# A fused attention and feed-forward kernel: its first batch gets a schedule of its own

## Chip, cores and metric

One core of a Trainium2 chip runs the kernel. The metric is the device time of one execution in microseconds, the median of repeated runs. Engines are called by the profile's names: PE is TensorE, DVE is VectorE, ACT is ScalarE, POOL is GpSimd, SP is SyncE, which here only issues DMAs.

## What is computed

Four batches (B = 4) of 448 positions (S), 12 heads (H) of 64 (D), in float32. Cut to what matters:

```python
scores = scale * np.matmul(q, k.transpose(0, 1, 3, 2))
scores = np.where(mask, -1000000000.0, scores)
scores = scores - np.max(scores, axis=-1, keepdims=True)
attn = np.exp(scores)
attn = attn / (np.sum(attn, axis=-1, keepdims=True) + 1e-09)
x = concat_heads(np.matmul(attn, v))
mu, var = mean(x), mean((x - mu) ** 2)
xn = (x - mu) / np.sqrt(var + 1e-06) * g_ln
out = x + np.maximum(xn @ w_ch1, 0.0) @ w_ch2
```

The mask is causal; the widths are 768 (x), 3072 (hidden) and 768.

## The kernel before

**The feed-forward part** (`ffn`) multiplies in three products of a rounded format: each weight tile is split into a high part `wh` and a rest `wl`, each input into `xh` and `xl` (later `hh` and `hl`), and `wh*xh`, `wh*xl` and `wl*xh` are summed in PSUM (L421, L440). It runs over 48 weight tiles a batch, in an order of slots: one slot is half of a pair of matmul groups. Weight tiles arrive packed; in the first batch ACT unpacks each with two instructions (L99, L103), DVE joins them (L110), ACT makes `wh` (L122) and DVE `wl` (L126), and the joined tile is kept in DRAM for the later batches (L117). All of these are the *conversions* of a tile.

**The attention part** works on pairs of heads (p = 0 to 5). Per pair: scores of row blocks of 112 (L227 for the first batch in plain float32, L234 for the others in rounded parts), a DVE instruction that adds the mask, scales and finds the row minimum of the negated scores (L242), ACT's exponential with row sums (L256), the normalization (r on DVE, L267 and L268, then four multiplications a head, L272), transposes of the probability blocks on PE into PSUM tile `pt` (L288), their copies to `PT` by ACT (L291) or DVE (L293), and the product with the values, `px` (L303), copied to `xT` (L307). When all six pairs are done, means and variances are taken (`stats`, L316 and L319; `aggr`), spread over the partitions by matmuls into `mb` and `rb` (`spread`, L336 and L341), and `xg`, `xh` and `xl` are made (L351 to L361).

**What sets the order.** Each engine runs its instructions in the order of the program, which is written out by slot numbers: `steps` puts each step of pair p at slot 6p plus a table value (SAT0 for scores, one slot later the exponentials, NAT0 for the normalization, TAT0 for transposes, END0 for the value product, TH0 for statistics). Attention of batch 1 to 3 runs in the slots of the feed-forward part of the batch before it; attention of batch 0 runs ahead of everything, in negative slots (the *head* below). EARLY, GAP and ELAG place the conversions of the first four weight tiles in the head. For batch 1, HOLE and FIRST pull the first steps into the head: the loads, splits and scores of its first pair.

In the head the queries and keys of a pair lie as three planes: head 0 in rows 0 to 63 with zeros below, head 1 in rows 64 to 127 with zeros above, and the keys of both; POOL writes the zeros (L171, L172). A scores matmul so runs over 128 rows, half of them zero. PSUM has eight banks, three named sc, two mm, two pt, one pv; scores of the head take turns over sc and mm. DMAs are all issued from SP's queue.

Of the kernel before, what the change touches and what calls it, by code (L numbers as in the profile page):

```python
# [40 lines left out]
NDVE = 7  # L41
# [6 lines left out]
def kernel(ctx, tc, qk, v, w1, w2, g, out):  # L48
# [108 lines left out]
    class Att:  # L157
# [47 lines left out]
        def scores(self, p, grp):  # L205
            if self.b == 0:
                tag, bufs = (("sc", 3), ("sc", 3), ("sc", 3), ("mm", 2), ("mm", 2))[self.turn % 5]
                self.turn += 1
            else:
                tag, bufs = "sc", 3  # L210
# [3 lines left out]
            for h, i in grp:  # L214
                n = C * (i + 1)
                if ("P", p, h) not in self.t:
                    x = 2 * p + h
                    if self.b == 0 and x % 5 >= 3:
                        a = 2 * NC * D * NP + (x % 5 - 3) * OFF[NC]
                        old = (x - 5) // 2, (x - 5) % 2  # L220
                        assert x < 5 or all(("T", *old, j) in self.done for j in range(NC))
                        self.t["P", p, h] = rest[:C, a:a + OFF[NC]]
                    else:
                        self.t["P", p, h] = sb.tile([C, OFF[NC]], F32, tag="P", name="P", bufs=3)
                if self.b == 0:
                    r = self.t["raw", p]
                    nc.tensor.matmul(  # L227
                        pt[:, o:o + n], lhsT=r[:, h, C * i:C * i + C], rhs=r[:, 2, :n],
                        start=True, stop=True,
                    )  # L230
                else:
                    qs, kh, kl = self.t["qk", p]
                    for kk, part in ((kh, 0), (kl, 1)):
                        nc.tensor.matmul(  # L234
                            pt[:, o:o + n], lhsT=qs[:, h, C * i:C * i + C], rhs=kk[:, h, :n],
                            start=(part == 0), stop=(part == 1),
                        )
# [12 lines left out]
        def exps(self, p, grp):  # L250
            nm = self.t.pop(("nm", p, tuple(grp)))
            for x, (h, i) in enumerate(grp):
                if ("sm", p, h) not in self.t:
                    self.t["sm", p, h] = sb.tile([C, NC], F32, tag="sm", name="sm", bufs=6)
# [7 lines left out]
        def norm(self, p, h):  # L262
# [6 lines left out]
            eng = nc.vector if self.b or p >= NDVE else nc.gpsimd  # L269
            for i in (0, 1, 3, 2):  # L270
                pp = self.t["P", p, h][:, OFF[i]:OFF[i + 1]]
                eng.tensor_scalar(  # L272
# [75 lines left out]
        def apply1(self, c):  # L348
# [4 lines left out]
            )  # L353
            nc.vector.scalar_tensor_tensor(
# [11 lines left out]
        def steps(self):  # L366
# [6 lines left out]

            if self.b == 0:
                sat, tat, nat, end, ev = SAT0, TAT0, NAT0, END0, EV0
            else:
                sat, tat, nat, end, ev = SAT, TAT, NAT, END, EV1 if self.b == 1 else EV
            period = 6
            for p in range(NP):
                t0 = period * p  # L380
                if self.b:
# [3 lines left out]
                for h in range(2):  # L385
                    put(pre, t0 + nat[h], self.norm, p, h)
                put(post, t0 + end, self.pv, p)
                for x, grp in enumerate(TGROUPS):
                    put(post, t0 + tat[x], self.transposes, p, grp, "act" if ev[x] else "dve")
                for x, grp in enumerate(SGROUPS):  # L390
                    put(post, t0 + sat[x], self.scores, p, grp)
                    put(pre, t0 + sat[x] + 1, self.exps, p, grp)
# [9 lines left out]
            for c in range(KC):  # L402
                x = c if self.b else c // 2
                put(pre, ta + 1 + x, self.apply1, c)
# [4 lines left out]
    def ffn(a, s, hh, hl):  # L409
        for f0, f1 in ((0, HF), (HF, NF)):  # L410
            for x in range(0, HF, 2):
# [4 lines left out]
                for k, (y, c) in enumerate(seq):  # L416
# [3 lines left out]
                    for i, (w, z) in enumerate(((wh[ws], a.xh), (wh[ws], a.xl), (wl[ws], a.xh))):  # L420
# [29 lines left out]
    with tc.manual_schedule():  # L450
        more_qk = sb.tile([P, KC, S], F32, tag="xh", name="more_qk", bufs=1)
        first_qk = sb.tile([P, HF, S], F32, tag="hh", name="first_qk")
        rest = sb.tile([P, HF * S], F32, tag="hl", name="rest")
        pre, post, att = {}, {}, {}

        def add_batch(b):
# [32 lines left out]
        for s in range(start, B * ns):  # L489
            for b in range(1, B):  # L490
                if b not in att and s >= (b - 1) * ns - (-start if b == 1 else 8):
# [49 lines left out]
```

## Time and profile before

| | before |
|---|---|
| median of 3 runs | 918.5 us (918.12 to 918.62) |
| the profiled execution, its own time | 920.24 us |
| span in its profile | 918.4 us |
| busy share of the span | PE 98%, DVE 60%, ACT 49%, POOL 13% |
| chain that ended last, by engine | PE 87%, ACT 6%, DVE 5% |
| first feed-forward matmul | starts at 79.18 us |

The profile is of one execution; times in it count from the start of its span. Busy time of PE is the modelled length of matmuls that overlap each other, so a PE row that is long may follow the last one sooner than its length says: the distance between starts is what counts. The granted clock is that of PE, 1.00 for 2.4 GHz and 0.50 for 1.2 GHz.

### The profile page before, as it was taken

Reading aid. Unit: us, or ns where it says so; the run is one execution under the profiler, and the core shown is the slowest. Engines: PE = TensorE matmul, PEld = TensorE weight load, DVE = VectorE, ACT = ScalarE, POOL = GpSimd, SP = SyncE. Lnnn points to the kernel's source line nnn. Section 1 sums busy time; section 2 is a strip of 40 time slices with the busy share of each in tenths; the row PEclk is TensorE's granted clock in tenths of the full one; section 3 lists DMA queues with packets and bytes.
Section 4 is the critical chain, followed back from the end, with each engine's and each line's share of the span. In section 5 each row is a group of like instructions: output and inputs, shape, how many; then the busy total and the mean of one; then the engine's idle time right before and its main releaser. Section 6 shows DMA issues by size and latency. Waiting matters only on the chain.

```text
span 918.4 us, 12826 instructions
## 1 busy us (share of the span) xinstructions
PE 897.3 (98%) x4864; PEld 790.0 (86%) x4864; DVE 554.0 (60%) x1208; ACT 452.8 (49%) x907; POOL 121.6 (13%) x115
## 2 busy tenths in 40 slices
PE   6988999999999999999999999999999999999998
PEld 4656889888899988988889998888988999999997
DVE  4877678777778566655664676556664634333431
ACT  5955788778865444444432355433542333222320
POOL 5543111001022111100102210011100200000000
PEclk9999999999999999999999999999999999999999
DMA  9921778887778643333213634343222343323210
GB/s 236 345 78 34 274 253 285 285 304 244 257 253 273 238 153 110 105 128 119 98 50 125 215 126 150 120 151 112 84 95 77 121 146 117 121 103 103 103 65 31
DMA packets 35247, 144.36 MB, mean 157 GB/s; under 512 B 4081, under 2 KB 8689, under 8 KB 35185
## 3 DMA queue, kind: packets, MB, share of 16 engines
q1 hardware_dynamic: 35184, 143.54, 45.3%
q8 instruction: 38, 0.62, 0.3%
q14 instruction: 25, 0.20, 0.1%
HBM read 119.15 MB, written 24.38 MB: 156 GB/s over the span
## 4 chain that ended last, share of the span: by engine, by line
PE 87%; ACT 6%; DVE 5%; DMA 1%; issue 1%; SPq 1%; POOL 0%; ACTq 0%
PE po L440 38%; PE ph L421 33%; PE px L303 5%; PE sc L234 4%; PE pt L288 4%; ACT P L256 2%; PE pln L316 1%; DMA raw<-w_dram 1%; ACT w L99 1%; ACT bits L103 1%; PE sc L227 1%; DVE hl L427 1%; ACT wh L122 1%; DVE P L272 1%; DVE wl L126 1%
## 5 line engine op out<-in xcount | busy, mean ns | idle before, releaser
L421 PE MATMUL ph<-xh,wh 128*128 128x448 f32 x576 | 214.5, 372 | 2.2 <-ACT xh L358 1.4
L440 PE MATMUL po<-hh,wh 128*128 128x448 f32 x576 | 214.1, 372 | 0.0
L421 PE MATMUL ph<-xl,wh 128*128 128x448 f32 x576 | 211.7, 367 | 0.8 <-POOL xl L361 0.8
L421 PE MATMUL ph<-xh,wl 128*128 128x448 f32 x576 | 211.5, 367 | 0.2
L440 PE MATMUL po<-hh,wl 128*128 128x448 f32 x576 | 210.7, 366 | 0.0
L440 PE MATMUL po<-hl,wh 128*128 128x448 f32 x576 | 210.6, 366 | 0.0
L427 DVE SCALAR_TENSOR_TENSOR hl<-ph,hh 128x448 fp32r<-128x448 f32 x96 | 59.9, 624 | 147.1 <-ACT hh L426 147.1
L122 ACT ACTIVATE wh<-full 128x768 fp32r<-128x768 f32 x144 | 119.3, 838 | 53.7 <-PE po L440 50.8
L126 DVE TENSOR_TENSOR wl<-full,wh 128x768 fp32r<-128x768 f32 x144 | 136.4, 954 | 0.8 <-ACT wh L122 0.5
L426 ACT ACTIVATE hh<-ph 128x448 fp32r<-128x448 f32 x96 | 52.0, 543 | 154.2 <-PE ph L421 154.1
L256 ACT ACTIVATE P<-P,nm 112x448 f32<-112x448 f32 (+3 forms) x176 | 91.8, 524 | 68.0 <-DVE nm L242 68.0
L421 PEld LDWEIGHTS ph<-xh,wh 128*128 128x128 f32 x576 | 108.7, 189 | 11.2 <-ACT xh L358 1.6
L421 PEld LDWEIGHTS ph<-xh,wl 128*128 128x128 f32 x576 | 108.6, 189 | 10.6 <-DVE wl L126 2.1
L421 PEld LDWEIGHTS ph<-xl,wh 128*128 128x128 f32 x576 | 108.7, 189 | 9.0 <-POOL xl L361 1.1
L440 PEld LDWEIGHTS po<-hh,wl 128*128 128x128 f32 x576 | 108.2, 188 | 9.3 <-DVE wl L126 0.4
L440 PEld LDWEIGHTS po<-hh,wh 128*128 128x128 f32 x576 | 108.2, 188 | 8.5
L440 PEld LDWEIGHTS po<-hl,wh 128*128 128x128 f32 x576 | 108.3, 188 | 8.1
L203 POOL TENSOR_TENSOR kl<-qkraw,kh 128x896 fp32r<-128x896 f32 x18 | 51.8, 2877 | 378.5 <-DVE kh L193 378.5
L242 DVE CUSTOM_DVE_ANT_0 P<-sc,mask 112x448 f32<-112x448 f32 (+3 forms) x176 | 70.6, 445 | 51.9 <-PE sc L234 39.7
L444 DVE TENSOR_TENSOR xT<-po,xT 128x448 f32<-128x448 f32 x48 | 29.9, 624 | 112.2 <-PE po L440 112.2
L288 PE MATMUL pt<-ident,P 112*112 112x112 f32 x440 | 55.3, 262 | 4.1 <-ACT PT L291 3.0
L288 PEld LDWEIGHTS pt<-ident,P 112*112 112x112 f32 x440 | 47.1, 134 | 13.9 <-ACT PT L291 4.6
(63 smaller groups left out, 940.6 us busy)
## 6 DMA issues: line engine op xcount, KB each, us to landing
full<-scratch SPq DMA_DIRECT2D x72, 768.0 KB, 4.3
raw<-w_dram SPq DMA_DIRECT2D x48, 768.0 KB, 5.6
scratch<-w SPq DMA_DIRECT2D x48, 384.0 KB, 2.9
qkraw<-qk_dram SPq DMA_DIRECT2D x18, 896.0 KB, 7.4
out_dram<-xT SPq DMA_DIRECT2D x24, 224.0 KB, 2.0
vt<-v_dram SPq DMA_DIRECT2D x18, 224.0 KB, 5.2
first_qk<-qk_dram SPq DMA_DIRECT2D x8, 224.0 KB, 5.9
rest<-v_dram SPq DMA_DIRECT2D x6, 224.0 KB, 8.2
```

Of the source, the lines that this page charges most:

```text
L122: nc.scalar.activation(out=wh[s], in_=w32[s], func=ACTF.Copy)
L126: nc.vector.tensor_tensor(out=wl[s], in0=w32[s], in1=wh[s].bitcast(F32), op=ALU.subtract)
L203: nc.gpsimd.tensor_tensor(out=kl, in0=rk, in1=kh.bitcast(F32), op=ALU.subtract)
L234: nc.tensor.matmul(pt[:, o:o + n], lhsT=qs[:, h, C * i:C * i + C], rhs=kk[:, h, :n], start=(part == 0), stop=(part == 1),)
L242: nc.vector.tensor_tensor_reduce(out=self.t["P", p, h][:, OFF[i]:OFF[i + 1]], in0=pt[:, o:o + n], in1=mask[:, S - n:], op0=ALU.add, op1=AL ...
L256: nc.scalar.activation(out=pp, in_=pp, func=ACTF.Exp, scale=-1.0, bias=nm[:, x:x + 1], accum_out=self.t["sm", p, h][:, i:i + 1],)
L288: nc.tensor.transpose(pt[:, o:o + C], pp[:, a:a + C], ident[:C, :C])
L303: nc.tensor.matmul(px[D * h:D * h + D, C * j:], lhsT=vt[:, h, j, :], rhs=self.t.pop(("PT", p, h, j)), start=(j == 0), stop=(j == NC - 1),)
L421: nc.tensor.matmul(pm[y], lhsT=w[:, c * P:c * P + P], rhs=z[:, c, :], start=(c == 0 and i == 0), stop=(c == KC - 1 and i == 2),)
L426: nc.scalar.activation(out=hh[:, x + y, :], in_=pm[y], func=ACTF.Relu)
L427: nc.vector.scalar_tensor_tensor(out=hl[:, x + y, :], in0=pm[y], scalar=0.0, in1=hh[:, x + y, :].bitcast(F32), op0=ALU.max, op1=ALU.subtract,)
L440: nc.tensor.matmul(pm, lhsT=w[:, o:o + P], rhs=z[:, x, :], start=(x == 0 and i == 0), stop=(x == HF - 1 and i == 2),)
```

## The change

1. First batch, scores: the zero planes and POOL's 12 memsets go. Head 0 lies in rows 0 to 63 and head 1 in rows 64 to 127 (queries and keys, two planes), and each scores matmul (L222 of the changed kernel) runs over its 64 rows; the two heads alternate and write two different PSUM tiles. The groups are block 3, blocks 0 and 2, block 1, of both heads.
2. First batch, order: new tables. One normalization for both heads (`norm0`) at slot 7 instead of two at slots 4 and 6, with r of 112x8; transposes from slot 9, value product at 14. A sixth buffer for probabilities (`more_p`). The second head of the last pair is normalized on DVE.
3. Conversions of the first four weight tiles: from slots -45, -39, -33, -27 to -15, -12, -9, -6, and closer to each other (ELAG).
4. Batch 1 loses HOLE and FIRST: all its steps stand where those of batches 2 and 3 stand, so its first pair's loads, splits and scores come after the start of the feed-forward part, and its other steps three slots later.
5. `apply1` is cut into `center` and `apply`; in batch 0 two centerings come ahead of two scalings. The second and third product of L421 change places.

```diff
-HOLE = [-7, 1]
-EARLY = 45
-GAP = 6
-FIRST = -20
-SAT0, TAT0, NAT0, END0, EV0 = [-1, 0, 2, 2, 4], [7, 8, 9, 10, 11], [4, 6], 13, [1, 1, 0, 1, 0]
+EARLY = 15
+GAP = 3
+GROUPS0 = [[3], [0, 2], [1]]
+SAT0, TAT0, NAT0, END0, EV0 = [0, 2, 4], [9, 9, 11, 11, 12], 7, 14, [0, 1, 0, 1, 0]
-TH0, TH = [38, 40], [18, 30]
-ELAG = [2, 5, 7]
+TH0, TH = [27, 39], [18, 30]
+ELAG = [1, 2, 3]
...
-                r = (first_qk if p < 4 else more_qk)[:, p % 4 * 3:p % 4 * 3 + 3, :]
-                nc.gpsimd.memset(r[D:, 0, :], 0.0)
-                nc.gpsimd.memset(r[:D, 1, :], 0.0)
-                nc.sync.dma_start(out=r[:D, 0:3:2, :], in_=qk[0, p][:D, 0:3:2, :])
-                nc.sync.dma_start(out=r[D:, 1:3, :], in_=qk[0, p][D:, 1:4:2, :])
+                r = first_qk[:, 2 * p:2 * p + 2, :]
+                nc.sync.dma_start(out=r[:D], in_=qk[0, p][:D, 0:3:2, :])
+                nc.sync.dma_start(out=r[D:], in_=qk[0, p][D:, 1:4:2, :])
...
+                for h in range(2):
+                    nc.tensor.matmul(
+                        tiles[h][:, o:o + n], lhsT=r[D * h:D * h + D, 0, C * i:C * i + C],
+                        rhs=r[D * h:D * h + D, 1, :n], start=True, stop=True,
+                    )
...
+        def norm0(self, p):
+            sm = self.t.pop(("sm", p))
+            r = sb.tile([C, 2, NC], F32, tag="r0", name="r0", bufs=2)
+            nc.vector.tensor_scalar_add(r, sm, 1e-9)
+            nc.vector.reciprocal(r, r)
+            for h in range(2):
+                eng = nc.vector if p == NP - 1 and h == 1 else nc.gpsimd
+                for i in (0, 1, 3, 2):
+                    eng.tensor_scalar(
...
-                    for i, (w, z) in enumerate(((wh[ws], a.xh), (wh[ws], a.xl), (wl[ws], a.xh))):
+                    for i, (w, z) in enumerate(((wh[ws], a.xh), (wl[ws], a.xh), (wh[ws], a.xl))):
...
-                if b != 1:
-                    return t + shift
-                if t < 0:
-                    return t + FIRST
-                return t - 2 + HOLE[0] if t <= 2 else t - 3 + HOLE[1]
+                return t + shift
```

**Place 1: DVE, from the transposes of one pair to the normalization of the next.** In the changed kernel, with `pt_237` and `pt_251` the last transposes of pair 0, `sc_258` and `sc_259` the first scores of pair 2, and `r0_266` the normalization of pair 1:

```order
L338 COPY PT_214<-pt_213 112x448
L232 ISA P_175,nm_231<-sc_227,mask_67 112x224
...
L338 COPY PT_238<-pt_237 112x448
L338 COPY PT_252<-pt_251 112x448
L232 ISA rest_97,nm_262<-sc_258,mask_67 112x448
...
L232 ISA rest_97,nm_264<-sc_259,mask_67 112x448
...
L257 TENSOR_SCALAR r0_266<-sm0_194 112x8
L258 RECIPROCAL r0_266<-r0_266 112x8
```

Before, each head has its own r, spread between the scores of the next pair, and conversions stand among them (`r_257` is the second pair's first head, `r_296` its second):

```order
L293 COPY PT_251<-pt_250 112x448
L267 TENSOR_SCALAR r_257<-sm_208 112x4
...
L293 COPY PT_286<-pt_285 112x448
L242 ISA rest_98,nm_293<-sc_292,mask_67 112x448
...
L267 TENSOR_SCALAR r_296<-sm_247 112x4
...
L126 TENSOR_TENSOR wl_305<-w32_193,wh_264 128x768
```

What moved: r of pair 1 now stands behind the masks of pair 2's first scores, for both heads at once.

**Place 2: PE in the same stretch of the changed kernel.** `P_136` and `P_138` are the probabilities of pair 0's two heads:

```order
L333 MATMUL pt_220<-ident_66,P_136 112x112 x4
L222 MATMUL sc_227<-first_qk_96 112x224
...
L333 MATMUL pt_237<-ident_66,P_136 112x112 x2
L333 MATMUL pt_237<-ident_66,P_138 112x112 x2
L333 MATMUL pt_244<-ident_66,P_138 112x112 x4
L333 MATMUL pt_251<-ident_66,P_138 112x112 x4
L222 MATMUL sc_258<-first_qk_96 112x448
L222 MATMUL sc_259<-first_qk_96 112x448
L348 MATMUL px_282<-PT_214,rest_97 64x448
```

What moved: the first scores of pair 2 stand behind all transposes of pair 0, and those behind the normalization of both its heads.

**Place 3: DVE between the last pair's normalization and the first feed-forward input**, in the changed kernel (`w32_651`, `w32_691`, `w32_743`, `w32_776` are the first four weight tiles):

```order
L258 RECIPROCAL r0_661<-r0_661 112x8
...
L108 SCALAR_TENSOR_TENSOR w32_651<-w32_651,bits_650 128x768
L124 TENSOR_TENSOR wl_688<-w32_651,wh_676 128x768
L338 COPY PT_695<-pt_694 112x448
...
L124 TENSOR_TENSOR wl_740<-w32_691,wh_720 128x768
L338 COPY PT_747<-pt_746 112x448
L364 BN_STATS stat_281<-pln_753 112x6
L108 SCALAR_TENSOR_TENSOR w32_743<-w32_743,bits_742 128x768
...
L108 SCALAR_TENSOR_TENSOR w32_776<-w32_776,bits_775 128x768
...
L371 BN_AGGR mv_792<-stat_281 112x2 x4
```

What moved: four joins and three `wl` instructions that stood earlier in the head are now between the last normalization and `aggr`, and each `wl` waits for an ACT instruction that waits for the join.

## Rows read from the trace of the kernel before

**Rows 1.** Busy time by stretch: PE, PEld, DVE, ACT, POOL, PE's clock, DMA share, GB/s

```profile
30.00:40.00 10.00, 10.00 (x65) 6.38 (x66) 8.68 (x32) 10.00 (x30) 6.88 (x12) 1.00 0.93 347
54.00:56.00 2.00, 2.00 (x10) 1.81 (x9) 0.44 (x4) 1.95 (x7) 1.60 (x4) 0.50 0.90 365
150.00:918.00 768.00, 764.60 (x4132) 688.10 (x4130) 448.27 (x916) 343.65 (x652) 71.12 (x36) 1.00 0.42 147
```

**Rows 2.** Timeline of PE, two pairs of the head: start, us, instruction, [idle before]

```profile
39.93 2.11 PE L303 MATMUL px<-PT,rest 112*64 112x448 f32 x16
41.97 0.98 PE L288 MATMUL pt<-ident,P 112*112 112x112 f32 x8
42.79 1.67 PE L227 MATMUL sc<-more_qk 128*112 128x224 f32 x6
...
46.50 1.68 PE L227 MATMUL sc<-more_qk 128*112 128x448 f32 x6
48.11 1.53 PE L303 MATMUL px<-PT,rest 112*64 112x448 f32 x6
52.07 1.16 PE L303 MATMUL px<-PT,rest 112*64 112x336 f32 x8 [2.43 <-DVE PT L293]
```

**Rows 3.** Timeline of DVE, the places that the sum uses

```profile
8.09 0.62 DVE L242 CUSTOM_DVE_ANT_0 P<-sc,mask 112x448 f32<-112x448 f32 x1 [8.09 <-POOL mhalf L485]
8.64 0.08 DVE L242 DVE_READ_ACCUMULATOR2_ANT nm<- 112x1 f32 x1
...
47.31 4.05 DVE L200 TENSOR_TENSOR qs<-qkraw,qs 64x896 fp32r<-64x896 f32 x1
...
58.64 0.16 DVE L267 TENSOR_SCALAR r<-sm 112x4 f32<-112x4 f32 x1
...
66.92 0.61 DVE L293 COPY PT<-pt 112x448 f32<-112x448 f32 x1
...
74.37 0.50 DVE L319 BATCH_NORM_STATS2 stat<-pln 112x6 f32<-112x128 f32 x2 [0.22 <-PE pln L316]
...
77.84 0.68 DVE L354 SCALAR_TENSOR_TENSOR xg<-xg,g_sb,rb 128x448 f32<-128x448 f32 x1 [0.98 <-PE rb L341]
```

**Rows 4.** Timeline of ACT, start of the head

```profile
8.76 0.67 ACT L256 ACTIVATE P<-P,nm 112x448 f32<-112x448 f32 x1 [6.74 <-DVE nm L242]
...
11.29 0.65 ACT L256 ACTIVATE P<-P,nm 112x448 f32<-112x448 f32 x1
...
15.03 0.96 ACT L99 ACTIVATE w<-raw 128x768 f32<-128x768 f32 x1 [2.06 <-DMA raw<-w_dram]
```

**Rows 5.** Timeline of POOL, the normalization of two heads in one piece

```profile
59.20 3.82 POOL L272 TENSOR_SCALAR P<-P,r 112x112 f32<-112x112 f32 x8 [3.60 <-DVE r L268]
```

**Rows 6.** Timeline of PE, first scores, one group of transposes, feed-forward start, batch 1

```profile
5.29 7.43 PE L227 MATMUL sc<-first_qk 128*112 128x448 f32 x22 [5.29 <-DMA first_qk<-qk_dram]
...
66.24 0.60 PE L288 MATMUL pt<-ident,P 112*112 112x112 f32 x4
...
90.61 0.47 PE L421 MATMUL ph<-xh,wh 128*128 128x448 f32 x1 [0.86 <-DVE hl L427]
...
105.39 0.46 PE L234 MATMUL sc<-kh,qs 128*112 128x448 f32 x1
...
106.40 0.36 PE L421 MATMUL ph<-xh,wh 128*128 128x448 f32 x1
```

**Rows 7.** Groups by line and shape, 0 to 80 us: busy us, mean ns | idle before

```profile
L110 DVE SCALAR_TENSOR_TENSOR w<-w,bits 128x768 uint32<-128x768 uint32 x4 | 3.8, 955 | 2.5 <-ACT bits L103 2.5
L126 DVE TENSOR_TENSOR wl<-w,wh 128x768 fp32r<-128x768 f32 x4 | 3.7, 928 | 0.0
L99 ACT ACTIVATE w<-raw 128x768 f32<-128x768 f32 x4 | 3.7, 921 | 2.1 <-DMA raw<-w_dram 2.1
L122 ACT ACTIVATE wh<-w 128x768 fp32r<-128x768 f32 x4 | 3.4, 853 | 0.0
```

**Rows 8.** Timeline of DVE, the same split of queries in batch 1's second pair

```profile
126.41 2.38 DVE L200 TENSOR_TENSOR qs<-qkraw,qs 64x896 fp32r<-64x896 f32 x1
```

**Rows 9.** Page, DMA issues: engine op xcount, KB each, us to landing

```profile
qkraw<-qk_dram SPq DMA_DIRECT2D x18, 896.0 KB, 7.4
```

More of the change, by code (lines that the diff above doesn't have):

```diff
@@ new lines, in exps0 @@
+        def exps0(self, p, grp):
+            if ("sm", p) not in self.t:
+                self.t["sm", p] = sb.tile([C, 2, NC], F32, tag="sm0", name="sm0", bufs=2)
+            for h in range(2):
+                nm = self.t.pop(("nm", p, h, grp[0]))
+                for x, i in enumerate(grp):
+                    pp = self.t["P", p, h][:, OFF[i]:OFF[i + 1]]
+                    nc.scalar.activation(
+                        out=pp, in_=pp, func=ACTF.Exp, scale=-1.0, bias=nm[:, x:x + 1],
+                        accum_out=self.t["sm", p][:, h, i:i + 1],
+                    )
+                    self.done.add(("exp", p, h, i))
@@ L211, in scores @@
+        def scores(self, p, grp):
+            tag, bufs = "sc", 3
             pt = ps.tile([C, S], F32, tag=tag, name="sc", bufs=bufs)
@@ L216, in scores @@
                 if ("P", p, h) not in self.t:
[L217 to L226, printed above, removed]
+                    self.t["P", p, h] = sb.tile([C, OFF[NC]], F32, tag="P", name="P", bufs=3)
+                qs, kh, kl = self.t["qk", p]
+                for kk, part in ((kh, 0), (kl, 1)):
                     nc.tensor.matmul(
-                        pt[:, o:o + n], lhsT=r[:, h, C * i:C * i + C], rhs=r[:, 2, :n],
-                        start=True, stop=True,
-                    )
[L231 to L237, printed above, removed]
+                        pt[:, o:o + n], lhsT=qs[:, h, C * i:C * i + C], rhs=kk[:, h, :n],
+                        start=(part == 0), stop=(part == 1),
+                    )
                 o += n
@@ L253, in exps @@
                 if ("sm", p, h) not in self.t:
[L254 removed]
+                    self.t["sm", p, h] = sb.tile([C, NC], F32, tag="sm", name="sm", bufs=4)
                 pp = self.t["P", p, h][:, OFF[i]:OFF[i + 1]]
@@ L372, in put @@
                 where.setdefault(t, []).append((f, a))
+            period = 6
             if self.b == 0:
-                sat, tat, nat, end, ev = SAT0, TAT0, NAT0, END0, EV0
-            else:
[L377 to L381, printed above, removed]
+                end = END0
+                for p in range(NP):
+                    t0 = period * p
+                    for x, grp in enumerate(GROUPS0):
+                        put(pre, t0 + SAT0[x] + 1, self.exps0, p, grp)
+                        put(post, t0 + SAT0[x], self.scores0, p, grp)
+                    put(pre, t0 + NAT0, self.norm0, p)
+                    for x, grp in enumerate(TGROUPS):
+                        put(post, t0 + TAT0[x], self.transposes, p, grp, "act" if EV0[x] else "dve")
+                    put(post, t0 + end, self.pv, p)
+            else:
+                end = END
+                for p in range(NP):
+                    t0 = period * p
                     put(pre, t0 - 4, self.load, p)
@@ L384, in steps @@
                     put(pre, t0 - 1, self.split2, p)
[L385 to L392, printed above, removed]
+                    for h in range(2):
+                        put(pre, t0 + NAT[h], self.norm, p, h)
+                    put(post, t0 + END, self.pv, p)
+                    for x, grp in enumerate(TGROUPS):
+                        e = (EV1 if self.b == 1 else EV)[x]
+                        put(post, t0 + TAT[x], self.transposes, p, grp, "act" if e else "dve")
+                    for x, grp in enumerate(SGROUPS):
+                        put(post, t0 + SAT[x], self.scores, p, grp)
+                        put(pre, t0 + SAT[x] + 1, self.exps, p, grp)
             tl = period * (NP - 1) + end + 1
@@ L490 @@
             for b in range(1, B):
-                if b not in att and s >= (b - 1) * ns - (-start if b == 1 else 8):
+                if b not in att and s >= (b - 1) * ns - 8:
                     assert add_batch(b) >= s, (b, s)
```

58 lines of the change are left out of this document (48 added, 10 removed).

## The prediction

> **What bounds the kernel now.** I read the busy table by stretches first. From 150 us to the end PE is busy 764.6 of 768 us [rows 1]: the feed-forward part is PE's, and whatever is added to PE there costs its full length. Only the head, ahead of it, can be shortened. As the mark between the two I take the start of the first scaling of `xg` at 77.84 us [rows 3]; from there 918.4 - 77.84 = 840.6 us follow.
>
> In the head, the second view is PE's timeline. From one value product to the next 48.11 - 39.93 = 8.2 us pass [rows 2], nearly all of it busy, and ACT is full too: both show 10.00 of 10 us [rows 1]. PE's 8.2 us are three pieces: the value products 41.97 - 39.93 = 2.0, twenty transposes (eight take 42.79 - 41.97 = 0.8, so 2.0), and the scores: 896 columns take 48.11 - 46.50 = 1.6 [rows 2], the 2240 columns of a pair 4.0. The value products stream 2240 columns as well, in half the time, since two heads use different columns of the array at once. So PE has something to gain from row halves: by that row, 4.0 would become about 2.3 (a pair of heads can overlap only from its second record on), and a pair would cost PE 6.3 us.
>
> The third view is what breaks the rhythm: the split of batch 1's queries holds DVE for 4.05 us [rows 3], PE stands 2.43 us behind it [rows 2], and afterwards its granted clock is 0.50 [rows 1]. At the start, DVE waits until 8.09 us for POOL's memsets [rows 3], though the first scores begin at 5.29 [rows 6], and ACT waits until 15.03 for a weight tile [rows 4].
>
> **Does the rhythm become 6.3 us? I say no.** In the changed order a new circle closes over PE, DVE and POOL: r of a pair, its normalization, the last transposes of that pair, the first scores of the pair two later, their masks on DVE, and only then r of the next pair. Its length, by rows: r to POOL's start 59.20 - 58.64 = 0.56 [rows 3, 5]; both heads on POOL 3.82 [rows 5]; the last two transposes of the third group until readable 0.5 (four take 66.92 - 66.24 = 0.68 to the start of their copy [rows 3, 6]); the copy 0.61 [rows 3], which frees the buffer of the last group; that group 0.4; the first scores 0.8, readable 0.2 later; two masks at 8.64 - 8.09 = 0.55 [rows 3], 1.1. Sum 8.0 us. PE's 6.3 us fit inside it, and so do ACT's: eight exponentials are twice what lies between 8.76 and 11.29 less one of 224 columns, 2 x 2.07 = 4.1 [rows 4], and three copies. The rhythm stays where it was, and PE idles a fifth of it. Row halves then give almost nothing: with the heads one after another the second tile would be readable 0.2 us later in the circle.
>
> **The head, added up.** r of the first pair needs all eight exponentials: scores from 5.29 [rows 6] at half clock (the 22 records there take 7.43 us; full clock by rows 2 would need some 5.6), first tile after 1.6, mask to exponential 8.76 - 8.09 = 0.7 [rows 3, 4], then 4.1: r at 11.8. The memsets no longer matter, since mask and identity come first on POOL. The next circle starts after an idle PE and gets 8.4: 20.2. Two of 8.0: 36.2. The fourth carries statistics of the first pairs, whose transposes use the same two buffers: two statistics and a transposition more on the path; 128 columns of statistics take 0.50/2 = 0.25 [rows 3], the 384 here some 0.55 by estimate, and three transposes of 128 columns 0.5 (four of 112 take 0.4): 1.6: 45.8. The last has no scores behind it (minus 2.1) but ends with a group and its copy (plus 0.9): 52.6.
>
> The tail, from the last r to the mark, on DVE's queue: r 0.4; four multiplications of the second head about 1.5 (POOL takes 3.82/2 for them [rows 5]); four joins 3.8 and three `wl` 2.8 [rows 7]; three copies 1.8 [rows 3]; statistics 4 x 0.25 [rows 3] and four of twice the width, 4 x 0.4 by estimate, 2.6; then what follows the last statistics now, 77.84 - (74.37 + 0.50) = 3.0 [rows 3]. That is 15.9, the lower bound. On top come waits: each `wl` for an ACT copy of 0.85 [rows 7] that itself waits for the join, and the last value product (2.0) with its copy, behind which the last statistics and, through two ACT instructions of 0.92 each [rows 7], the fourth join stand. I count 3.6 of 2.6 + 2.5, since copies and joins fill the rest: 19.5. The mark comes at **72.1, 5.7 us earlier**. The upper bound of the tail is 22, if none of the waits is filled.
>
> **What the feed-forward part takes on.** The scores of batch 1's first pair move behind the mark. A block row of 896 columns in both parts takes 106.40 - 105.39 = 1.0 [rows 6]; the pair has two and a half such, **2.4**: PE has no room there, so all of it counts. Before, four of its transposes filled the gap ahead of 90.61 [rows 6]; now they run elsewhere, **0.4**. In that gap the second matmul pair waits for DVE, and the queries' split now stands there, while POOL makes `xl`. The row for such a split beside POOL is 2.38 [rows 8], its worst 4.05 [rows 3]; it takes the place of a normalization and two r's, so I add **0.5**, bounds 0 and 2. The fourth `wl` amid the scalings adds 0.2, since centering ahead fills the wait for `rb`. Later slots, the three slots' shift and the exchanged products cost nothing: PE covers them, as it does for batches 2 and 3; without that cover each late conversion would cost 0.9. DMAs are the same bytes; SP issues the last of four packed tiles and batch 1's queries only after the fourth join, some 10 us before ACT needs them, against the 7.4 us to landing of such a load [rows 9].
>
> Sum: -5.7 + 2.4 + 0.4 + 0.5 + 0.2 = -2.2. On the profiled span 916.2; that execution took 920.24 with a span of 918.4, while the median is 918.5, so the difference is what I carry over: **916.3 us**. About 0.2% (1.8 us) is what a measurement of this kernel can tell from no change.
>
> **A rule against it.** Eight transposes last 0.98 us by their row, and the next work starts 0.82 after them [rows 2]: a record that had to let the array empty first would cost up to 0.16. By the Trainium skill, "TensorEngine Tiling (Array Packing)", Key Properties, a change of tiling mode drains TensorE, and the half-row scores change it twice a group. No row here shows such a change on row halves; the value products change columns, and their neighbours in rows 2 follow without a gap. One such change lies in the circle, five times: 0.8 us, 917.1 by that rule.
>
> **Rivals.**
> - *PE sets the pace.* If the circle is shorter than I add, the rhythm falls to 6.3 to 6.8 us, four circles gain about 1.3 each: 911. For it: with the conversions gone from the middle, DVE (8.68 of 10 us now) and POOL (6.88) have room [rows 1]. Against: each link of the circle has its row. 0.17.
> - *The clock falls in the tail, slower.* After 2.43 us of idle PE the granted clock was 0.50 [rows 1, 2]. In the new tail PE has some 4 us of transposes and statistics in 11. At half clock the last value product takes 2.0 more, the groups of transposes on the path 1.0, the means' broadcast 1.1: 4.1 in all, 920.4. It decides from 4.0 us on: beyond that nothing of the gain outlasts the measurement's 1.8. For it: the row. Against: the work is spread, not absent. 0.23.
> - *Row halves do not overlap, or drain.* The change then does not do what it says: PE 4 us a pair again, inside 8; 0.2 + 0.16 in five circles: 918.1. 0.10.
>
> **How the numbers follow.** The forecast, 0.50, has its own range 913.5 to 919 (tail 16.7 to 22); of it 0.30 lies below 916.7, 0.18 within 0.2%, 0.02 above. The first rival is faster (0.17), the second slower (0.23), the third within (0.08) or slower (0.02). Together: faster 0.47, same 0.26, slower 0.27. For 8 in 10 the range goes from 909.5 to 921.5.
>
> **What would show it.** Right: value products in the changed head 8 us apart, PE idle in each of them, waiting for POOL's normalization; DVE idle ahead of the masks of block 3; scores of 896 columns for both heads in little over half the time; first `xg` scaling near 72; no 4 us stall on DVE around 50; 2.4 us more of rounded scores behind it. Wrong: value products 6.5 us apart; the first scaling before 68 or after 76; scores no faster than now; PE waiting for DMA or `wl` in the first slots.

## The result: slower, and the profile after

The changed kernel takes 927.84 us (median of 4 runs, 927.64 to 928.35), the kernel before 918.31 beside it: a ratio of 1.0106 [1.0089, 1.0124], 1% slower where 0.2% faster was forecast. Its profiled execution takes 928.35 us with a span of 926.6. The mark (start of the first scaling) stands at 79.44 us instead of the forecast 72.1, and behind it 926.6 - 79.44 = 847.2 us follow instead of 844.1: 7.3 of the miss of 10.4 us lie in the head, 3.1 behind it.

The first view is the timeline of DVE: the normalizations (r) of the six pairs, and the mark. It answers to [rows 3].

```profile
11.33 0.17 DVE L257 TENSOR_SCALAR r<-sm 112x8 f32<-112x8 f32 x1 [0.66 <-ACT P L247]
...
21.40 0.17 DVE L257 TENSOR_SCALAR r<-sm 112x8 f32<-112x8 f32 x1
...
30.29 0.17 DVE L257 TENSOR_SCALAR r<-sm 112x8 f32<-112x8 f32 x1
...
39.86 0.17 DVE L257 TENSOR_SCALAR r<-sm 112x8 f32<-112x8 f32 x1
...
50.47 0.15 DVE L257 TENSOR_SCALAR r<-sm 112x8 f32<-112x8 f32 x1
...
57.29 0.16 DVE L257 TENSOR_SCALAR r<-sm 112x8 f32<-112x8 f32 x1
...
79.44 1.27 DVE L402 SCALAR_TENSOR_TENSOR xg<-xg,g_sb,rb 128x448 f32<-128x448 f32 x2 [0.56 <-PE rb L386]
```

The rhythm is 10.1, 8.9, 9.6, 10.6 and 6.8 us, and the tail from the last r to the mark 22.15. What closes the circle is seen in one timeline of all engines, around the fifth r:

```profile
45.62 0.47 ACT L247 ACTIVATE extra<-extra,nm 112x224 f32<-112x224 f32 x1
...
45.95 0.59 PE L333 MATMUL pt<-ident,P 112*112 112x112 f32 x4 [0.42 <-DVE stat L364]
...
46.47 0.54 PE L361 MATMUL pln<-ident,xT 128*112 128x128 f32 x3
...
47.22 0.60 PE L333 MATMUL pt<-ident,P 112*112 112x112 f32 x4 [0.21 <-ACT PT L336]
47.74 1.01 PE L222 MATMUL sc<-first_qk 64*112 64x448 f32 x4
...
48.69 0.54 PE L361 MATMUL pln<-ident,xT 128*112 128x128 f32 x3
48.89 0.62 DVE L232 CUSTOM_DVE_ANT_0 rest<-sc,mask 112x448 f32<-112x448 f32 x1 [0.42 <-PE sc L222]
...
49.44 0.62 DVE L232 CUSTOM_DVE_ANT_0 rest<-sc,mask 112x448 f32<-112x448 f32 x1
...
50.47 0.15 DVE L257 TENSOR_SCALAR r<-sm 112x8 f32<-112x8 f32 x1
...
51.05 1.93 POOL L264 TENSOR_SCALAR P<-P,r 112x112 f32<-112x112 f32 x4 [6.76 <-ACT rest L247]
```

The last exponential of the pair that r belongs to starts at 45.62 and takes 0.47, so its sums are there soon after 46; r starts at 50.47, since it stands on DVE's queue behind the masks of the next-but-one pair's first scores (48.89, 49.44), which wait for PE's scores (47.74), which stand behind the last transposes. POOL was idle for 6.76 us meanwhile. The row shows no wait ahead of r: the 4 us are in the order, not in a semaphore of r's own.

The third view is busy time by stretch (columns as in [rows 1]): the clock is at half where PE had paused shortly before, in the first circle, in the third and in most of the tail.

```profile
15.00:20.00 5.00, 5.00 (x20) 2.69 (x20) 1.96 (x6) 1.98 (x6) 0.76 (x2) 0.50 1.05 294
36.00:38.00 2.00, 1.96 (x9) 1.09 (x8) 0.62 (x1) 0.53 (x1) 0.00 (x0) 0.50 0.00 0
40.00:50.00 10.00, 8.53 (x64) 4.86 (x62) 6.67 (x25) 5.71 (x20) 3.83 (x8) 1.00 0.01 2
64.00:78.00 14.00, 11.30 (x48) 7.13 (x47) 8.21 (x20) 6.77 (x9) 1.03 (x1) 0.50 0.68 222
```

PE's timeline in the tail and at the start of batch 1's work, against [rows 2, 6]: the last value product takes 4.00 us instead of 2.11, and the scores of batch 1's first pair, now in the feed-forward part, wait for `kl`.

```profile
67.90 4.00 PE L348 MATMUL px<-PT,rest 112*64 112x448 f32 x16
...
91.24 0.37 PE L280 MATMUL sc<-kh,qs 128*112 128x448 f32 x1
92.56 0.47 PE L280 MATMUL sc<-kl,qs 128*112 128x448 f32 x1 [0.95 <-POOL kl L201]
...
106.43 0.40 PE L333 MATMUL pt<-ident,P 112*112 112x112 f32 x2 [0.36 <-DVE P L317]
107.30 0.47 PE L481 MATMUL ph<-xh,wl 128*128 128x448 f32 x1 [0.24 <-DVE wl L124]
```

### The profile page after: what moved, and what is told of

Read it like the earlier page. It is cut to its first block, busy times and chain, and to the rows that moved or that the text cites. A ratio compares the mean times of both kernels' runs of the same rounds, so it can differ in the third digit from the quotient of the medians.

```text
span 926.6 us, 12795 instructions
## 1 busy us (share of the span) xinstructions
PE 900.6 (97%) x4864; PEld 786.1 (85%) x4864; DVE 551.0 (59%) x1206; ACT 451.5 (49%) x901; POOL 114.5 (12%) x99
## 4 chain that ended last, share of the span: by engine, by line
PE 83%; DVE 8%; ACT 5%; POOL 2%; DMA 1%; issue 1%; SPq 0%; ACTq 0%; DVEq 0%; POOLq 0%
PE po L500 36%; PE ph L481 31%; PE px L348 5%; PE pt L333 4%; PE sc L280 4%; DVE wl L124 1%; PE sc L222 1%; ACT P L302 1%; DVE w L108 1%; PE pln L361 1%; DVE hl L487 1%; ACT wh L120 1%; DVE P L317 1%; DVE qs L198 1%; DMA vt<-v_dram 1%
## 5 line engine op out<-in xcount | busy, mean ns | idle before, releaser
L302 ACT ACTIVATE P<-P,nm 112x448 f32<-112x448 f32 (+3 forms) x144 | 75.1, 523 | 56.8 <-DVE nm L288 56.8
L288 DVE CUSTOM_DVE_ANT_0 P<-sc,mask 112x448 f32<-112x448 f32 (+3 forms) x144 | 57.2, 444 | 37.9 <-PE sc L280 37.9
L333 PEld LDWEIGHTS pt<-ident,P 112*112 112x112 f32 x420 | 45.2, 135 | 16.1 <-POOL P L264 5.8
```

What stands on the lines that cost most here:

```text
L288: nc.vector.tensor_tensor_reduce(out=self.t["P", p, h][:, OFF[i]:OFF[i + 1]], in0=pt[:, o:o + n], in1=mask[:, S - n:], op0=ALU.add, op1=AL ...
L302: nc.scalar.activation(out=pp, in_=pp, func=ACTF.Exp, scale=-1.0, bias=nm[:, x:x + 1], accum_out=self.t["sm", p, h][:, i:i + 1],)
L333: nc.tensor.transpose(pt[:, o:o + C], pp[:, a:a + C], ident[:C, :C])
```

## The experiments

Three causes were in question. Theory 1: r's place in DVE's order makes the circle long. Theory 2: batch 1's first pair costs more in the feed-forward part than the 2.4 us of its scores. Theory 3: PE's pauses bring the clock down, and that costs the rest. The rival to all: the conversions, pressed into the tail, are what costs. Every experiment is read at the same places: first r, the sum of the five circles, the tail up to the mark, the mark, and what follows it (span less mark), each from the rows of its own profiled execution, which can lie over a microsecond from the median of its kernel (experiment 4: 923.58 against 924.94). *Circles* is the sum of the five distances from one r to the next. Each ratio is to runs of the kernel before on the same chip:

| kernel | first r | circles | tail | mark | after mark | median | ratio to before |
|---|---|---|---|---|---|---|---|
| before | | | | 77.84 | 840.6 | | 1 |
| forecast | 11.8 | 40.8 | 19.5 | 72.1 | 844.1 | 916.3 | |
| the change | 11.3 | 46.0 | 22.2 | 79.4 | 847.2 | 927.84 | 1.0106 |
| 1: r one slot earlier | 11.3 | 41.0 | 21.9 | 74.1 | 847.6 | 923.6 | 1.0049 [1.0033, 1.0065] |
| 2: PE kept busy | 11.3 | 43.4 | 20.9 | 75.6 | 847.1 | 924.56 | 1.0059 [1.0044, 1.0074] |
| 3: conversions back | 11.4 | 53.2 | 17.2 | 81.8 | 846.1 | 929.79 | 1.0118 [1.0098, 1.0139] |
| 4: pair back | 11.8 | 46.0 | 23.9 | 81.6 | 840.2 | 924.94 | 1.006 [1.0045, 1.0075] |
| 5: 1 and 4 | 11.4 | 41.5 | 23.7 | 76.6 | 841.3 | 919.6 | 1.0008 [0.9999, 1.0017] |
| 6: 5, second head on DVE | 11.4 | 52.6 | 24.4 | 88.4 | 840.7 | 930.45 | 1.0124 [1.0108, 1.0139] |
| 7: heads in turn | 11.3 | 43.8 | 21.6 | 76.7 | 847.6 | 926.7 | 1.0085 [1.0071, 1.0099] |
| 8: second head on DVE | 11.4 | 43.5 | 22.0 | 76.9 | 847.8 | 927.6 | 1.01 [1.0083, 1.0117] |
| 9: 5, PE kept busy, old order of products | 11.7 | 41.7 | 24.4 | 77.7 | 839.7 | 919.41 | 1.0007 [0.9996, 1.0017] |
| 10: 5, heads in turn, old order of products | 11.5 | 43.0 | 23.8 | 78.2 | 840.7 | 920.17 | 1.0013 [1.0004, 1.0022] |
| 11: 5, conversions back | 11.3 | 49.8 | 19.9 | 81.0 | 841.1 | 924.31 | 1.006 [1.0047, 1.0072] |
| 12: before, one instruction moved | | | | 74.8 | 840.6 | 916.96 | 0.9977 [0.9965, 0.9989] |

### 1. r one slot earlier

```diff
-SAT0, TAT0, NAT0, END0, EV0 = [0, 2, 4], [9, 9, 11, 11, 12], 7, 14, [0, 1, 0, 1, 0]
+SAT0, TAT0, NAT0, END0, EV0 = [0, 2, 4], [9, 9, 11, 11, 12], 6, 14, [0, 1, 0, 1, 0]
```

> The changed kernel with the normalization one slot earlier (NAT0 = 6), so that r of a pair no longer stands on DVE behind the masks of the first scores two pairs on. Circle theory: r follows r after about 5.6 to 6.8 us instead of 8.9 to 10.6, value products come 6.5 to 7 us apart, the first xg scaling moves from 79.4 to 71 to 74 and the time from 927.8 to about 920 to 922; with less idle time PE's clock stays at 1.00 in the middle of the head. Rival, the clock alone makes the head slow: value products stay 8 us or more apart, under 2 us gained. Rival, TensorE's own work sets the pace: no more than 1 us gained.

One digit takes 5.3 us off the mark and 4 to 5 off the time. DVE and POOL in the circle that was shown above:

```profile
43.75 0.15 DVE L257 TENSOR_SCALAR r<-sm 112x8 f32<-112x8 f32 x1
...
44.34 1.93 POOL L264 TENSOR_SCALAR P<-P,r 112x112 f32<-112x112 f32 x4 [6.08 <-DVE r L258]
...
45.00 0.62 DVE L232 CUSTOM_DVE_ANT_0 rest<-sc,mask 112x448 f32<-112x448 f32 x1 [0.31 <-PE sc L222]
```

r now stands ahead of the masks (43.75 against 45.00), and POOL scales while PE still computes the scores. Theory 1 holds in its direction, but its size was overrated: value products were expected 6.5 to 7 us apart and stand 6.9 to 10.6 apart, the mark is just past the expected 71 to 74, and the time is 923.6 instead of 920 to 922. Part of the 5.3 us is the clock, which stays at 1.00 in the third circle here. What r's place is worth by itself shows against experiment 2, where the third circle also runs at full clock. The value products around that circle, of this run and then of experiment 2:

```profile
26.93 2.11 PE L348 MATMUL px<-PT,rest 112*64 112x448 f32 x16
...
34.78 2.11 PE L348 MATMUL px<-PT,rest 112*64 112x448 f32 x16
```

```profile
27.01 2.11 PE L354 MATMUL px<-PT,rest 112*64 112x448 f32 x16
...
35.84 2.11 PE L354 MATMUL px<-PT,rest 112*64 112x448 f32 x16
```

They are 7.85 us apart here and 8.83 there (9.99 in the changed kernel). From the first to the fifth value product 33.2 us pass here and 35.3 there: some 2 us for r's place as such.

### 2. PE kept busy

Matmuls of 448 columns ahead of batch 0's transposes, into the PSUM tile that these overwrite. The edit adds 14 of them (four for the first pair, one for each of the next four, six for the last), not the 16 that the expectation names:

```diff
+            for _ in range(fill):
+                nc.tensor.matmul(pt, lhsT=ident[:C, :C], rhs=mask, start=True, stop=True)
```

> The changed kernel with 16 extra matmuls (identity times mask, 0.75 us at full clock) written into the PSUM tiles that transposes of the first batch overwrite: three ahead of the first pair's transposes, one ahead of each later pair's, seven among the last pair's. They do nothing but keep PE busy where it waits. Clock theory: granted clock at or near 1.00 from 12 to 79 us, circles of 10.1 and 9.6 us fall to 8.0 to 8.5, the tail (r of the last pair to the first xg scaling, 22.2 us) to 19 to 20.5, in all 4 to 6 us faster than the changed kernel, 922 to 924. Rival, the low clock is only seen there and sits beside waits: no gain, or up to 5 us slower by the added matmuls.

They add work to PE, and the kernel gets 3 to 4 us faster (span 926.6 to 922.7), a little less than the 4 to 6 expected; what follows the mark is unchanged. Busy time by stretch (the clock falls late in the last one all the same):

```profile
15.00:20.00 5.00, 4.67 (x29) 2.39 (x28) 3.17 (x11) 2.24 (x7) 0.69 (x2) 1.00 1.05 298
36.00:38.00 2.00, 2.00 (x18) 1.02 (x18) 1.46 (x6) 1.23 (x4) 0.26 (x1) 1.00 0.00 0
64.00:78.00 14.00, 8.82 (x46) 5.80 (x46) 9.75 (x22) 6.53 (x10) 2.03 (x2) 0.83 0.80 279
```

Circles one and three, the two that ran in part at half clock, fall from 10.07 and 9.57 to 8.63 and 8.41, the tail from 22.15 to 20.91: the clock cost at least 3.8 us of the mark, since the fillers' own time is not taken off.

### 3 and 4. The two moves undone, one at a time

Experiment 3 puts the conversions back:

```diff
-EARLY = 15
-GAP = 3
-ELAG = [1, 2, 3]
+EARLY = 45
+GAP = 6
+ELAG = [2, 5, 7]
```

> The changed kernel with the conversions where they were before (EARLY 45, GAP 6, ELAG 2, 5, 7). Theory: the tail loses its four conversions and shrinks from 22.2 to 15 to 18 us, but two of DVE's conversion instructions stand right behind r in each circle and slow POOL's normalization from 3.8 to some 5 us, so that circles grow by about 1.3 us each: net between 3 us faster and 2 us slower than the changed kernel's 927.8. Rival, late conversions are the main cost of the change: 5 us faster or more. Rival, they hide: within 1 us.

Experiment 4 puts all steps of batch 1 back, its first pair into the head and the others three slots earlier:

```diff
+HOLE = [-7, 1]
+FIRST = -20
...
-                return t + shift
+                if b != 1:
+                    return t + shift
+                if t < 0:
+                    return t + FIRST
+                return t - 2 + HOLE[0] if t <= 2 else t - 3 + HOLE[1]
...
-                if b not in att and s >= (b - 1) * ns - 8:
+                if b not in att and s >= (b - 1) * ns - (-start if b == 1 else 8):
```

> The changed kernel with batch 1's first steps back in the head (HOLE and FIRST as before, for every batch-1 step). Theory: the stretch from the first hl to the end of the first batch's feed-forward part, 5.7 us longer than before in the changed kernel, loses 2.4 us of scores, 0.4 of transposes and 0.95 of waiting for kl, 3.5 to 5 us; but in the head the queries' split stands on DVE beside POOL's normalization and costs 2 to 4 us there, and the scores fill PE's idle tail. Net 0 to 3 us faster, 925 to 928. Rival, the moved pair explains most of the loss: 5 us or more faster. Rival, it is hidden: no change.

With the conversions back the tail loses 5.0 us and the circles grow by 7.2: their place in the tail was not the loss, and the rival falls. With the pair back everything behind the mark is as before (840.2 against 840.6), and the mark comes 2.2 later. So the move of batch 1's steps cost 7.0 us in the feed-forward part, more than the 3.5 to 5 expected, for 2.2 in the head; between experiments 1 and 5, where r is early, it is 6.2 for 2.4. The first pair's move and the three slots' shift of the other steps were undone together, so how the 7.0 divide between them is not shown. The conversions' new place and the new order of the products together leave nothing behind the mark.

### 5. Both edits together; 6 and 8. Half of the normalization off POOL

```diff
-                eng = nc.vector if p == NP - 1 and h == 1 else nc.gpsimd
+                eng = nc.vector if h == 1 else nc.gpsimd
```

Experiment 5 is 1 and 4 together; 6 adds this edit to it, 8 makes this edit alone.

> The two edits that helped most, together: the normalisation one slot earlier, and the second batch's first pair back at its old place. Alone they took 4.8 and 4.6 us off the span of the changed kernel (926.6 to 921.7 and to 921.8), the one before the mark (start of the first scaling), the other mostly behind it. Theory A, each works in its own stage (circle; FFN of the first batch): they add up, 927.8 - 9.4 = 918.4, level with the kernel before (ratio 0.998 to 1.002). Rival B, both are the same slack, since the pair's scores now stand in the pauses that the earlier normalisation removes: only half of the second gain comes, 920 to 922 (ratio 1.002 to 1.004).

> The kernel of the run with both edits, and in it the second head's normalisation of every pair on DVE instead of POOL, so that POOL's part of the circle falls from 3.83 to 1.93 us. Theory A, the circle with POOL in it sets the rhythm: up to 1.9 less in each of four circles, less 0.8 that the second head's four scalings take on DVE: 3 to 6 us faster than the run with both edits, 913 to 915. Rival B, with r ahead of the next pair's masks POOL is no longer what ends the circle (PE and the DVE evictions are): 917.5 to 918.5, no gain.

> The changed kernel with only the second head's normalisation moved from POOL to DVE. Theory A, POOL's 3.83 us stand in every circle: 1.9 less in four circles, less up to 0.8 on DVE: 4 to 7 us faster, 921 to 924. Rival B, the 0.8 us on DVE stand ahead of the next masks and take the gain back: 926 to 928.

Experiment 5 adds up (theory A) and is level with the kernel before: the two edits account for the whole loss. In the changed kernel (experiment 8) the halving moves the time by nothing that can be told, which is rival B. On top of experiment 5 (experiment 6) it costs 11 us, which neither theory had. The timeline of experiment 8 says why nothing is won:

```profile
29.32 1.87 DVE L264 TENSOR_SCALAR rest<-rest,r 112x112 f32<-112x112 f32 x4
...
29.45 2.15 POOL L264 TENSOR_SCALAR rest<-rest,r 112x112 f32<-112x112 f32 x4 [6.14 <-DVE r L258]
```

A head takes 1.87 us on DVE (0.8 was assumed) and 2.15 on POOL beside it; DVE gives up in its queue what POOL saves. Experiment 6 shows a collision, in DVE, POOL and PE:

```profile
48.92 4.81 DVE L266 TENSOR_SCALAR extra<-extra,r 112x112 f32<-112x112 f32 x4
49.08 2.07 POOL L266 TENSOR_SCALAR P<-P,r 112x112 f32<-112x112 f32 x4 [8.90 <-DVE r L260]
...
51.12 2.06 POOL L203 TENSOR_TENSOR kl<-qkraw,kh 128x896 fp32r<-128x896 f32 x1
...
55.57 2.50 PE L350 MATMUL px<-PT,rest 112*64 112x336 f32 x10 [4.18 <-DVE PT L340]
```

The four scalings last 4.81 us and end at 53.73, 0.55 behind POOL's `kl` (51.12 + 2.06); PE stands 4.18 us behind them. That circle takes 15.5 us instead of 8.4; the other four are 0.7 to 1.2 longer each.

### 7. Heads in turn

```diff
-            for i in grp:
-                n = C * (i + 1)
-                for h in range(2):
+            for h in range(2):
+                o = 0
+                for i in grp:
+                    n = C * (i + 1)
```

> The changed kernel with the two heads of a pair scored one after the other instead of alternately, so that the two row halves no longer overlap; nothing else is touched. By the record, 896 columns of scores then take 1.6 us instead of 0.95. Theory A, the scores lie in the circle between the last transposes and the masks: 0.65 for a group of 896 columns in it, two groups a pair, five circles: 3 to 6 us slower than the changed kernel, 931 to 934. Rival B, as the prediction had it, PE waits for the normalisation anyway, and the time stays within 1 us of 927.8.

It is no slower, if anything faster; neither theory holds. The premise was wrong, as PE's timeline of this run shows (eight records, 896 columns in all, and what starts after them):

```profile
21.32 1.03 PE L223 MATMUL sc<-first_qk 64*112 64x112 f32 x8
22.27 0.40 PE L334 MATMUL pt<-ident,P 112*112 112x112 f32 x2
```

0.95 us, as in the changed kernel (22.73 to 23.68), against 1.6 over 128 rows [rows 2], though in the program a head's two blocks now follow each other. The single records of the trace say why: they still start in pairs, one of each head, 0.013 us apart (0.007 in the changed kernel). So the two row halves overlap in either order, and the edit did not take away the overlap that it was meant to take away. What the overlap is worth for the time is therefore not measured. (For blocks 3 and 1 the edit alters nothing, one matmul a head.) What differs ahead of the mark are above all the first and the third circle, 9.16 and 8.38 against 10.07 and 9.57; the third has no stretch at half clock this time. The pause of PE in it is the same, in the changed kernel and then in this run:

```profile
32.84 0.79 PE L333 MATMUL pt<-ident,rest 112*112 112x112 f32 x6 [0.83 <-POOL rest L264]
```

```profile
31.82 0.79 PE L334 MATMUL pt<-ident,rest 112*112 112x112 f32 x6 [0.82 <-POOL rest L265]
```

So the same pauses bring the clock down in one execution and not in another.

### 9, 10 and 11. On the base of experiment 5

Experiment 9 has the fillers of experiment 2, two more ahead of the means' broadcast, and the old order of the three products:

```diff
+            for _ in range(0 if self.b else 2):
+                nc.tensor.matmul(mb[:C], lhsT=ident[:C, :C], rhs=mask, start=True, stop=True)
...
-                    for i, (w, z) in enumerate(((wh[ws], a.xh), (wl[ws], a.xh), (wh[ws], a.xl))):
+                    for i, (w, z) in enumerate(((wh[ws], a.xh), (wh[ws], a.xl), (wl[ws], a.xh))):
```

Experiment 10 has that order and the edit of experiment 7 (which leaves the overlap here too), 11 the edit of experiment 3.

> The kernel with both edits (919.6), the old order of the three products of the FFN, and matmuls on TensorE where it pauses (16 ahead of transposes as in the filler run, and two ahead of the means' broadcast), whose results are overwritten. Theory A, what is left of the loss is the clock: the record of the run with both edits has the granted clock at half from 14 to 17 us, 62 to 65.3 and 72 to 85; with it kept up the value product, the broadcast (3.9 against 2.3 us) and the first products (0.57 against 0.37 us, 20 of them) give back 3 to 5 us, the order of the products 0.6 to 1: 914 to 916.5, ratio 0.994 to 0.998. Rival B, the fillers take as much of TensorE's time (0.83 us each) as the clock gives back: 918 to 919.

> The kernel with both edits, the old order of the three products, and the heads of a pair scored in turn, so that nothing of the row halves' overlap is left. Theory A, the overlap buys nothing because TensorE then pauses and its clock falls: 0 to 2 us faster than the run with both edits, of which 0.6 to 1 is the order of the products: 917.5 to 919. Rival B, with the earlier normalisation TensorE is nearer to the pace, and 0.65 us a group count: 921 to 924.

> Of the whole change only the first batch's own schedule and its row halves: the first four conversions and the second batch's pair are where they were before, and the normalisation one slot earlier. Theory A, the conversions cost as much in the attention as at its end, so that their move was worth little: in the changed kernel their return cost 1 to 2 us, here the same: 920.5 to 921.5. Rival B, with the earlier normalisation DVE's and ACT's 0.93 us a conversion stand ahead of r and of the exponentials in each circle: 923 to 926. Rival C, they fill pauses now, and the tail falls by the 5 us that the return gave there: 914 to 917.

In experiment 9 the clock stays at 1.00 from 14 to 80 us, and still the circles do not change (41.7 against 41.5) and the tail is 0.7 longer (rival B, if a little above its 918 to 919): with r early, PE's speed is no longer what the circle waits for. So the gains of experiments 1 and 2 are not to be added: with PE kept busy in both, the early r takes 1.7 off the circles (43.4 in experiment 2, 41.7 here, with the pair back as well). Against experiment 5, both 9 and 10 gain 0.6 us between the seventh and the 25th `hl` instruction (0.57 and 0.61): that is the order of the products, at the low end of what was expected. Behind the mark as a whole, where experiment 4 is level with the kernel before, something else gives as much back. Experiment 10 lies between its theories. In experiment 11 the tail falls by 3.8 and the circles grow by 8.3 (rival B), 3.3 of it through the same collision as above, now with a conversion:

```profile
53.13 4.28 DVE L126 TENSOR_TENSOR wl<-w,wh 128x768 fp32r<-128x768 f32 x1
...
54.52 2.07 POOL L203 TENSOR_TENSOR kl<-qkraw,kh 128x896 fp32r<-128x896 f32 x1
```

So under the new schedule the conversions are better off in the tail. The schedule with row halves, its normalization early and the conversions where they were, is 0.6% slower than the kernel before.

### 12. The collision in the kernel before

The 4.05 us query split that the prediction read [rows 3] has the same shape, so one instruction of the kernel before was moved:

```diff
-            nc.gpsimd.tensor_tensor(out=kl, in0=rk, in1=kh.bitcast(F32), op=ALU.subtract)
+            eng = nc.vector if self.b == 1 and p == 0 else nc.gpsimd
+            eng.tensor_tensor(out=kl, in0=rk, in1=kh.bitcast(F32), op=ALU.subtract)
```

> The kernel before, and in it one instruction of the second batch's first pair moved: the subtraction that makes kl, from POOL to DVE (behind the query split, about 1.1 us there). In the record of before that query split took 4.05 us on DVE (47.31 to 51.36) while POOL scaled and subtracted, against 1.09 in the run with both edits; TensorE then waited 2.43 us for the eviction behind it and 3.0 us later for another. Theory A, POOL's subtraction beside it stretched the split: split and subtraction together now take 2.2 to 2.8 us, the waits of 2.43 and 3.0 shrink by 1.5 to 3 us, and the time falls to 916 to 917.5 (ratio 0.997 to 0.9985), the fastest of all kernels here. Rival B, the scaling on POOL alone stretches the split, or the circle takes the gain back: 918 to 919.5.

Theory A, in time and in rows of DVE and PE:

```profile
46.03 1.48 DVE L200 TENSOR_TENSOR qs<-qkraw,qs 64x896 fp32r<-64x896 f32 x1
...
47.54 1.32 DVE L204 TENSOR_TENSOR kl<-qkraw,kh 128x896 fp32r<-128x896 f32 x1
...
49.45 1.35 PE L304 MATMUL px<-PT,rest 112*64 112x336 f32 x10 [1.11 <-DVE PT L294]
```

Split and subtraction take 2.8 us together where the split alone took 4.05; PE waits 1.11 instead of 2.43, and the mark comes at 74.8 instead of 77.84. Of these 3.0 us the medians show 2.0 (the profiled execution of the kernel before took 920.24 us, more than its median). At 916.96 us this is the fastest kernel here, 0.23% ahead of the kernel before.

## Why the prediction was wrong

**What held.** The feed-forward part is PE's. The circle that the prediction closed over PE, DVE and POOL is what paces the changed head, and the rhythm did not fall to 6.3, although row halves do what they should on PE (0.95 us for 896 columns; a pair about 2.45 where 2.3 was forecast and 4.0 stood before). That they give almost nothing is not shown: no run has scores over 128 rows in the new order. First r came at 11.3 against 11.8 (its terms add up to 11.7). The wait of 0.95 for `kl` lies where the prediction saw a risk, though it is not the split that is late (1.12 us): POOL starts `kl` only at 89.68, behind the last `xl`, and needs 2.82 us. The 4.05 us stall is gone. The rule of the Trainium skill, "TensorEngine Tiling (Array Packing)", Key Properties, that was weighed at 0.8 us did not show ahead of the scores: four transposes ahead of row-half scores pass in 47.74 - 47.22 = 0.52 us, four ahead of 128-row transposes in 46.47 - 45.95 = 0.52. For the change back, behind the scores, no row gives a comparison.

**The term of the circles: 40.8 against 46.0.** The prediction added 8.0 from rows at full clock, and only the start at less. Experiment 2 splits the 5.2: 2.6 are the clock, 2.6 remain with PE kept busy, some of it the fillers' own. The step that failed is "PE idles a fifth of it", taken as harmless: PE's pauses brought the clock down in the middle of the head, though not in every execution (experiment 7). Of the other 2.6, 1.1 lie in the circle with the statistics (10.69 in experiment 2, against 9.6). The prediction also did not ask whether r had to stand there; experiment 1 takes 5.0 off with one slot, some 2 by r's place and the rest with the clock.

**The term of the tail: 19.5 against 22.15.** Its bound of 22 "if none of the waits is filled" is what came. Of the 2.65, 1.2 go with the clock by experiment 2; the rival "the clock falls in the tail" had the mechanism (4.00 us for the value product, 2.0 more, as it said) and a chance of 0.23, but was priced for the tail alone, and there at 4.1, of which experiment 2 shows 1.2. On DVE, two `wl` wait 0.91 each for ACT:

```profile
60.93 0.96 DVE L124 TENSOR_TENSOR wl<-w,wh 128x768 fp32r<-128x768 f32 x1 [0.91 <-ACT wh L120]
...
70.31 0.96 DVE L124 TENSOR_TENSOR wl<-w,wh 128x768 fp32r<-128x768 f32 x1 [0.91 <-ACT wh L120]
```

**The feed-forward part: +3.5 against +6.6.** The failed step is "Later slots, the three slots' shift and the exchanged products cost nothing: PE covers them". The scores' 2.4 and the transposes' 0.4 are still counted. To them come the wait for `kl`, 0.95 where 0.5 was added for the split, and short waits that the prediction put at nothing. From the waits table of PE, 92 to 303 us (us in total, times, longest):

```profile
PE pt L333 <- DVE P L317: 1.1, 3, 0.4
PE sc L280 <- POOL kl L201: 0.9, 1, 0.9
PE ph L481 <- DVE wl L124: 0.7, 3, 0.2
```

With the pair back in the head (experiment 4) the normalization's waits there fall to 0.4, those for `wl` to 0.2, and none is for `kl`. The kernel before also waits 0.4 for the normalization, so 0.7 of the 1.1 are new. Together 2.4 + 0.4 + 0.95 + 0.7 + 0.7 = 5.15 of 6.6; of the other 1.4, 1.0 comes in small steps behind the 25th `hl` instruction. It goes with the pair as well and was not taken apart. The exchanged products cost 0.6 by experiments 9 and 10, not nothing, though the time behind the mark shows no more than the pair's part.

Sum: 2.6 (clock) and 2.6 in the circles, 1.2 (clock) and 1.4 in the tail, less 0.5 at the start: 7.3 to the mark; 3.1 behind it: the 10.4 us. The range's upper end, 921.5, took the bad cases one at a time; here the clock in the circles, the clock in the tail and the waits behind the mark came together.

## What to carry to other kernels

When a circle over several engines sets the pace, look at what stands ahead of its first instruction on an in-order queue: r was ready for 4 us and waited for another pair's masks, with no wait in its row. Shortening PE's work where PE is not last buys pauses, and pauses can cost clock (2.6 us of the circles here), so price the whole stretch at half clock as a case of its own. A step that an engine seems to have room for next to a saturated one is worth moving only after its releasers' queues have been followed: here 7.0 us of loss for 2.2 of gain.

## What the runs showed of the hardware

DVE and POOL hold each other up on work in SBUF. Three different pieces of DVE work stretched to the same picture beside POOL's subtraction for `kl`: the query split 4.05 us (1.09 in experiment 5), a conversion 4.28 (0.93 elsewhere [rows 7]), four scalings 4.81 (1.87 beside a scaling on POOL), each ending 0.55 to 0.94 us after `kl` did. With `kl` off POOL (experiment 12) the split takes 1.48. Where the split comes first (experiment 5) it is POOL that waits: its four scalings beside the split take 2.71 us, the next four 1.91. DVE's masks, which read PSUM, are not touched; in experiment 5:

```profile
49.26 0.50 DVE L234 CUSTOM_DVE_ANT_0 rest<-sc,mask 112x336 f32<-112x336 f32 x1
49.67 2.09 POOL L203 TENSOR_TENSOR kl<-qkraw,kh 128x896 fp32r<-128x896 f32 x1
...
49.88 0.50 DVE L234 CUSTOM_DVE_ANT_0 rest<-sc,mask 112x336 f32<-112x336 f32 x1
```

By the Trainium skill, "SBUF — State Buffer", section "SBUF: two separate sides", DVE and GpSimd share one pair of ports as an exclusive lock, and the one that comes second fully blocks, if the DVE instruction reads two inputs from SBUF or runs in a mode that uses both ports. The rows agree with it: the split and the conversion have two inputs in SBUF, the masks one (the other is in PSUM). Which mode the scalings ran in no run shows. One thing more stands in the rows: the conversion began at 53.13, ahead of `kl` at 54.52, and still ended behind it, so POOL's next instruction went first.

Float32 scores over 64 rows take 0.95 us for 896 columns against 1.6 over 128, whether or not the program alternates the two halves: their records start 0.007 to 0.013 us apart in both orders. And the granted clock fell to half beside pauses of PE of less than 2 us each: ahead of the stretch from 15 us PE had waited 1.60 and 0.83 us for POOL and was busy for 1.46 us from 10 to 14 us. From 40 to 50 us, with PE busy for 8.53 of 10 us, it stayed at 1.00, and after the same pause in the third circle it fell in the changed kernel and stayed up in experiment 7.
